# Strassen products for pairs of token chunks in a fused attention and Mish MLP kernel

## The chip, the cores and the metric

One core of a Trainium2 chip. The metric is the device time of one execution in microseconds (us), as the median of several runs. A core has TensorE (PE, matmuls; PEld is its weight load), VectorE (DVE), ScalarE (ACT), GpSimd (POOL) and SyncE (SP, which here only issues DMAs), 16 DMA engines, the on-chip memory SBUF and the matmul result memory PSUM (8 banks of 128 x 512 f32).

## The reference

```python
scores = scale * q @ k.T + bias          # 8 batches, 8 heads, 576 tokens, head size 64
mask = (rel >= 0) & (rel < 128)          # a sliding window of 128 tokens
attn = softmax(where(mask, scores, -1e9))
x = (attn @ v), heads side by side       # 4608 tokens x 512
h = x @ w_in                             # 512 x 2048, float64 weights
g = h * tanh(softplus(h))                # Mish
return g @ w_out                         # 2048 x 512, float64 weights
```

## The kernel before, in words

The 4608 tokens are nine chunks of 512: the first 512 tokens of each of the eight batches (chunks 0 to 7), and chunk 8 of the eight left-over groups of 64. A chunk c has a **first product** (`first`, L407), h = x W_in, in eight pieces j of 256 of the 2048 columns: each is a PSUM tile `h` of [128, 2, 512] with tag "s" (two such buffers, four banks), filled by 24 matmuls and emptied by one ScalarE Mish into `g`. It has a **second product** (`second`, L459), g W_out, in 2 halves x 8 pieces x 2 row blocks of six matmuls each, accumulated in PSUM `po0` and `po1` and stored by `store` (L472).

For precision every operand is a sum of a high and a low part (float32r): a product is three passes, high x high, high x low, low x high. The parts of x come from `split_hi` on ScalarE and `split_lo` on VectorE (L277, L282), those of g from `parts` (L425: ScalarE's high part, GpSimd's low part). W_in and W_out come as float64 words and are turned into parts once, during chunk 0's first product (`sign_w`, `bits_w`, `high_w`, `low_w`, L149 to L174: ScalarE, VectorE, ScalarE, VectorE); all parts then stay in SBUF, in tiles `wi0` to `wi7` and `wo0` to `wo7` of 8 KB per partition.

Attention of a batch is four head pairs p, each with two `unit`s (halves, L185) and a `last_unit` (L302, the 64 left-over tokens). A unit goes through `scores` (PE), `peak` (VectorE: window and maximum), `exps` (ScalarE), `sums` (VectorE), `scale` (GpSimd), `weights` (PE transposes, then VectorE's masking copy), `values` (PE), then the split of x. The left-over tokens go to DRAM (`xs`) and come back as chunk 8 (`last_x`, L391).

Every engine runs its instructions in the order in which they are emitted (`InOrder`, L20). That order is written by hand: lists of (time, step) are sorted by time and emitted. From chunk 1 on, the first product of a chunk stands alone (L523 to L528); beside its 32 steps of the second product (integer times, six matmuls each) stand the attention steps of the next chunk (L543 to L544), four head pairs eight steps apart, at the times that `unit` returns (L296 to L300), multiplied by 4:

```python
(0, scores), (0.02 + t, peak), (0.026 + 27 * t, exps), (0.27 + 33 * t, sums),
(0.33 + 33 * t, scale), (1.53, weights), (1.99, values), (2.02, split_hi), (2.02, split_lo),
```

so that six steps of the second product stand between a unit's scores and its transposes. Loads and stores are issued on SP in the same manner.

Of the kernel before, what the change touches and what calls it, by code (L numbers as in the profile page):

```python
# [16 lines left out]
P = 128  # L17
# [20 lines left out]
def attention_mish_mlp(  # L38
# [132 lines left out]
    def low_w(kind, j):  # L171
        ready.add((kind, j))
        w, t = wt[(kind, j)], wv.pop((kind, j))
        dve.tensor_tensor(out=w[:, 1, :], in0=t, in1=w[:, 0, :].bitcast(F32), op=ALU.subtract)  # L174
# [3 lines left out]
        n = 256 if kind == "i" else DM  # L178
        return wt[(kind, j)][:, part, c * n : c * n + n]

    xt = {}

    HEAD = [slice(i * D, (i + 1) * D) for i in range(2)]

    def unit(b, p, half):  # L185

# [88 lines left out]
                        skip_group_check=True,  # L275
                    )
        def split_hi():  # L277
            if half == 1:
                x = xt[(b, p)] = xp.tile([P, 2, CH], F32R, tag=f"x{p}", name=f"x{b}_{p}")
                act.activation(x[:, 0, :], qkv[("o", b, p)], AF.Copy)  # L280

        def split_lo():  # L282
            if half == 1:
# [12 lines left out]
        t = 0.01 * half  # L296
# [5 lines left out]
    def last_unit(b, p):  # L302

        st = {}
        name = f"{b}_{p}l"
# [61 lines left out]
        if b == 0:  # L367
# [2 lines left out]
                (2.19, keep),  # L370
            ]
        return [
            (0.01, scores), (0.04, peak), (0.31, exps), (0.5, sums), (0.5, scale), (1.54, weights), (1.995, values), (1.996, keep),
        ]

    def attention(b):

        steps = []
        for p in range(NP):
            units = [(2 * p, unit(b, p, 0)), (2 * p, last_unit(b, p)), (2 * p + (b == 0), unit(b, p, 1))]
            steps += [(k + d, f) for k, u in units for d, f in u]
            nxt = (b, p + 2) if p + 2 < NP else (b + 1, p + 2 - NP)
            if 0 < nxt[0] < B:
                steps.append((2 * p + 1.03, lambda nxt=nxt: load_qk(*nxt)))
                steps.append((2 * p + 3.01 - (b > 0), lambda nxt=nxt: load_v(*nxt)))
        return sorted(steps, key=lambda s: s[0])

    def last_x():  # L391
        c = B
        for p in range(NCC):
            raw = at.tile([P, 1024], F32, tag="pz", name=f"xr{p}")[:, :CH]
            sp.dma_start(out=raw, in_=xs[p])
            x = xt[(c, p)] = xp.tile([P, 2, CH], F32R, tag=f"x{p}", name=f"x{c}_{p}")
            act.activation(x[:, 0, :], raw, AF.Copy)
            ready.add((c, p))
            dve.tensor_tensor(
                out=x[:, 1, :], in0=raw, in1=x[:, 0, :].bitcast(F32), op=ALU.subtract  # L400
            )

    gt = {}

# [15 lines left out]

    gs = {}

    def parts(c, half, j):  # L425
# [4 lines left out]
        act.activation(gh, src, AF.Copy)  # L430
        pool.tensor_tensor(out=gl, in0=src, in1=gh.bitcast(F32), op=ALU.subtract)
        gs[(c, half, j)] = (gh, gl)

    po = {}

# [35 lines left out]

    def store(c, half, t):  # L472
        ob = out_tile(c, half, t)
        queues = [sp, sp]
        if (c, half, t) == (B, 1, 1):
            queues = [sp, act]
            act.activation(ob[:, : DM // 2], po[t][:, : DM // 2], AF.Copy)
            dve.tensor_copy(ob[:, DM // 2 :], po[t][:, DM // 2 :])
        elif t == 0:
            dve.tensor_copy(ob, po[t])  # L480
        else:
            act.activation(ob, po[t], AF.Copy)
        for q, (k, rows) in zip(queues, rows_of(c, 2 * half + t)):
            q.dma_start(out=rows, in_=ob[k])

    ORDER = [("i", j) for j in range(NJ)] + [("o", j) for j in range(NJ)]
    LATE = ORDER[-1:]
# [3 lines left out]

    UNIT, START, SLOT = 4.1, 4.7, 5.45
    X0 = START + 9.0 * UNIT
    steps = [(START + UNIT * t, f) for t, f in attention(0)]
# [25 lines left out]
    for _, work in sorted(steps, key=lambda s: s[0]):  # L520
        work()

    for c in range(B + 1):  # L523
        for j in range(NJ if c else 0):
            if j == NJ - 1:
                parts(c, 0, 0)
                parts(c, 0, 1)
            first(c, j)()  # L528

        n = 4 * NJ  # L530
        steps = []
        for m in range(2 * NJ):
            for t in range(2):
                steps.append((2 * m + t, lambda m=m, t=t: second(c, *divmod(m, NJ), t)))
                if m % NJ == NJ - 1:
                    late = 2 if m == n // 2 - 1 and c + 1 < B else 0
                    steps.append((2 * m + t + late, lambda m=m, t=t: store(c, m // NJ, t)))
            if m >= 2:
                steps.append((2 * m - 4.1, lambda m=m: parts(c, *divmod(m, NJ))))
        for w, times in zip(LATE, ((2.3, 8.4, 8.5, 8.9),) if c == 0 else ()):  # L540
            for f, t in zip((sign_w, bits_w, high_w, low_w), times):
                steps.append((t, lambda f=f, w=w: f(*w)))
        if c + 1 < B:  # L543
            steps += [(4 * s + 0.8, f) for s, f in attention(c + 1)]  # L544
        elif c + 1 == B:
            steps.append((4.5, last_x))
        for _, work in sorted(steps, key=lambda s: s[0]):
            work()


_INS = ["q", "k", "v", "moe_w_in", "moe_w_out"]
# [82 lines left out]
```

## Time and profile before

| | us |
|---|---|
| median of 3 runs | 988.91 (988.65 to 989.43) |
| the profiled execution | 988.93 |
| its span, first to last instruction | 987.2 |
| PE busy in the span | 974.5 |

The profile is of one execution; the time of the execution is its span and some 1.7 us around it. "Busy" counts the time in which an engine executes, and matmuls overlap in PE's pipeline. Rows name line 30 for nearly all work, since a helper there records every operation: go by tile names (`h` first product, `po` second product, `s`, `o`, `pt` attention, `gs` parts of g, `si` and `so` parts of the weights, `pz` a unit's exponentials).

### The profile page before, as it was taken

The numbers are of one execution on the slowest core, as the hardware profiler recorded it, in microseconds if no ns is written. First come the engines' busy times: TensorE is split into PE (matmuls) and PEld (weight loads), VectorE is DVE, ScalarE is ACT, GpSimd is POOL, SyncE is SP. The second block draws the span as 40 slices with busy tenths as digits, with TensorE's granted clock in tenths as the row PEclk, the third lists the DMA queues.
The fourth block names the chain that finished last, engine by engine and source line by source line (L and its number), as shares of the span: only waits on it lengthen the run. The fifth ranks groups of instructions, "written<-read, shape, count | busy, mean of one in ns | idle before, by whom it ended". The sixth has DMA issues, their size and how long they took to land.

```text
span 987.2 us, 13729 instructions
## 1 busy us (share of the span) xinstructions
PE 974.5 (99%) x5325; PEld 786.2 (80%) x5329; DVE 322.6 (33%) x1120; ACT 361.2 (37%) x900; POOL 256.0 (26%) x228
## 2 busy tenths in 40 slices
PE   8999999999999999999999999999999999999998
PEld 4678788888888888888888888888888888888886
DVE  6889651044401541055302540145204440000000
ACT  4785541244314332253314531344124431331221
POOL 3210540035103340144104330154004510250142
PEclk9999999999999999999999999999999999999999
DMA  9930131012200221021200310013101110000001
GB/s 374 426 153 28 53 94 37 1 52 81 78 1 27 78 69 37 1 69 65 76 1 28 105 54 25 26 54 95 37 0 51 55 46 1 22 22 21 1 11 33
DMA packets 23393, 61.31 MB, mean 62 GB/s; under 512 B 6688, under 2 KB 7840, under 8 KB 21280
## 3 DMA queue, kind: packets, MB, share of 16 engines
q1 hardware_dynamic: 22016, 59.65, 17.7%
q8 instruction: 42, 0.69, 0.3%
q10 hardware_dynamic: 1312, 0.79, 0.3%
q14 instruction: 23, 0.19, 0.1%
HBM read 49.94 MB, written 10.49 MB: 61 GB/s over the span
## 4 chain that ended last, share of the span: by engine, by line
PE 91%; DVE 4%; ACT 2%; issue 2%; POOL 0%; POOLq 0%; DVEq 0%; ACTq 0%
PE po L30 39%; PE h L30 35%; PE s L30 8%; PE o L30 5%; PE pt_1l L30 1%; PE pt_2l L30 1%; DVE so L30 1%; PE pt_3l L30 1%; DVE ti L30 1%; PE pt_0l L30 1%; DVE to L30 1%; DVE si L30 1%; PE idle L30 1%; ACT wo L30 1%; DVE pz L30 1%
## 5 line engine op out<-in xcount | busy, mean ns | idle before, releaser
L30 PE MATMUL po<-so,gs 128*128 128x512 f32 x1728 | 409.7, 393 | 0.0
L30 PE MATMUL h<-x,si 128*128 128x512 f32 x1728 | 395.3, 390 | 1.6 <-DVE si L30 0.9
L30 PEld LDWEIGHTS h<-x,si 128*128 128x128 f32 x1728 | 323.4, 188 | 70.6 <-DVE si L30 1.7
L30 PEld LDWEIGHTS po<-so,gs 128*128 128x128 f32 x1728 | 320.4, 188 | 65.5
L30 POOL TENSOR_TENSOR gs<-g,gs 128x512 fp32r<-128x512 f32 x144 | 186.3, 1300 | 674.2 <-ACT gs L30 651.3
L30 ACT ACTIVATE g<-h 128x1024 f32<-128x1024 f32 x72 | 74.0, 1027 | 268.2 <-PE h L30 268.2
L30 ACT ACTIVATE gs<-g 128x512 fp32r<-128x512 f32 x144 | 89.4, 628 | 130.7 <-PE po L30 130.7
L30 DVE COPY_PREDICATED s<-older,s 128x256 f32<-128x256 uint16 x64 | 35.6, 557 | 276.6 <-PE s L30 276.6
L30 ACT ACTIVATE pz<-pz,mx 128x128 f32<-128x128 f32 x256 | 99.5, 391 | 44.8 <-DVE mx L30 43.9
L30 DVE TENSOR_TENSOR pz<-s,masks 128x1024 f32<-128x1024 f32 x56 | 66.0, 1219 | 70.1 <-PE s L30 69.6
L30 POOL TENSOR_TENSOR pz<-pz,sm 128x512 f32<-128x512 f32 x64 | 66.7, 1042 | 37.9 <-DVE sm L30 27.6
L30 DVE CUSTOM_DVE_ANT_0 pz<-s,nb 128x128 f32<-128x128 f32 x256 | 59.1, 287 | 2.8
L30 PE MATMUL s<-qk 64*128 64x256 f32 (+1 forms) x512 | 59.1, 368 | 0.0
L30 DVE COPY ob<-po 128x512 f32<-128x512 f32 (+1 forms) x19 | 12.8, 674 | 136.6 <-PE po L30 135.5
L30 ACT ACTIVATE x<-o 128x512 fp32r<-128x512 f32 x32 | 19.0, 594 | 102.2 <-PE o L30 102.2
L30 PE MATMUL o<-pz,va 128*64 128x128 f32 (+1 forms) x560 | 48.7, 320 | 0.0
L30 ACT ACTIVATION_READ_ACCUMULATOR pz<-pz,mx 128x1 f32 x256 | 48.3, 189 | 0.0
L30 PEld LDWEIGHTS s<-qk 64*128 64x128 f32 x512 | 41.6, 189 | 8.3 <-issue 2.1
L30 PEld LDWEIGHTS o<-pz,va 128*64 128x64 f32 x560 | 33.7, 136 | 18.2 <-issue 7.5
L30 PE MATMUL s<-ident,pz 128*128 128x128 f32 x256 | 34.4, 274 | 1.8 <-POOL pz L30 1.8
L30 PEld LDWEIGHTS s<-ident,pz 128*128 128x128 f32 x256 | 29.4, 141 | 7.4 <-POOL pz L30 3.0
L30 ACT ACT_TABLE_LOAD x17 | 21.8, 1283 | 11.2 <-DVE mx L30 11.1
(118 smaller groups left out, 371.4 us busy)
## 6 DMA issues: line engine op xcount, KB each, us to landing
qk<-in_qk_dram SPq DMA_DIRECT2D x31, 640.0 KB, 4.7
va<-in_v_dram SPq DMA_DIRECT2D x28, 320.0 KB, 3.1
wi<-in_moe_w_in_dram SPq DMA_DIRECT2D x8, 1024.0 KB, 12.5
wo<-in_moe_w_out_dram SPq DMA_DIRECT2D x8, 1024.0 KB, 19.9
out_dram<-ob SPq DMA_DIRECT2D x32, 256.0 KB, 2.0
qk<-in_v_dram SPq DMA_DIRECT2D x4, 320.0 KB, 5.8
xr<-xs SPq DMA_DIRECT2D x4, 256.0 KB, 2.7
out_dram<-ob SPq DMA_DIRECT2D x7, 128.0 KB, 2.3
```

Source lines behind the costliest of these rows:

```text
L30: ins = method(*args, **kwargs)
```

## The change

The first products of chunks 1 to 8 are made for pairs (1,2), (3,4), (5,6), (7,8). With X cut into the two chunks and two halves of its 512 features, and W_in into two halves of each side, the eight block products become seven (Strassen's scheme in Winograd's form): X11 W11, X12 W21, four products of sums, and one of a sum with W22. Each is 8 column blocks of 128 x 2 row blocks x 3 passes of matmuls of 128x512. Results are combined as they are evicted (`product`). The W_in sums S1 to S4 are made once, by GpSimd, from W_in parts written to DRAM during chunk 0; all W_in operands of the products are then streamed from DRAM, in 1 MB tiles, through three SBUF buffers per pair. The rest of the W_in tiles become result buffers. Chunk b of a pair keeps its x unsplit (`raw_x`) for the sums. Attention of both chunks of a pair stands beside the second products of the pair before; those of chunks 1 and 2 both stand beside chunk 0's second product and the first two products, with their own times (`FORM[0]`). The diff, cut:

```diff
@@ weights and split
+        elif kind == "i" and j in (3, 5, 7):
+            t = ff.tile([P, 1024], F32, tag="g", name=f"t{kind}{j}", bufs=3)
...
+        if kind == "i" and j > 1:
+            (act if j < 4 else sp).dma_start(out=whole[j], in_=t)      # in bits_w
...
+            if half == 1 and b in raw_x:
+                act.activation(raw_x[b][:, p, :], qkv[("o", b, p)], AF.Copy)
...
-            (0, scores), (0.02 + t, peak), (0.026 + 27 * t, exps), (0.27 + 33 * t, sums),
-            (0.33 + 33 * t, scale), (1.53, weights), (1.99, values), (2.02, split_hi), (2.02, split_lo),
+            (0.8, scores), (0.88 + 0.04 * t, peak), (0.9 + 1.08 * t, exps), (total[half], sums),
+            (total[half] + 0.01, scale), (turn[half], weights), (give[half], values), (give[half] + 0.12, split_hi),
+            (low, split_lo),
...
+        if w[0] == "i":
+            steps.append((lows[n] + 2, lambda j=w[1]: sp.dma_start(out=wr[j], in_=wt[("i", j)].bitcast(F32))))
@@ the pairs
+    PAIRS = [(c, c + 1) for c in range(1, B + 1, 2)]
+    FORM = [   # starts of the head pairs, then turn, give, total, low
+        ((0, 5, 11, 16, 22, 27, 33, 38), (3.15, 4.05), (5.14, 5.16), (0.94, 3.0, 3.1), 6.6),
+        (range(0, 64, 8), (6.92, 6.92), (8.76, 8.78), (1.88, 3.2, 2.8), 8.9),
+    ]
+    COMBINE = (
+        (4.95, 5.3, 5.35, 9.15, 9.4, 14.3, 10.3, 15.15, 16.75, 15.2, 15.95, 17.55),
...
+    )
+    WHOLE = ((4.15, 4.2), (9.2, 9.95))
+    PARTS = (0.1, 3.7, 5.0, 5.5, 8.9, 10.9, 11.5, 15.0, 16.3, 19.7, 21.0, 22.5, 25.1, 26.6)
+    PROD = ["11", "12", "S1", "S2", "S4", "S3", "22"]
...
+    def whole_w(j, k):                       # 4 calls
+        pool.tensor_tensor(out=cw[j][:, 0, k], in0=cw[j][:, 0, k], in1=cw[j][:, 1, k], op=ALU.add)
+    def combine(j):                          # j 0 to 3: four adds, two high, four low, two saves
+        def add(out, x, y, op):
+            pool.tensor_tensor(out=out, in0=x, in1=y, op=op)
+        def high(w):
+            act.activation(w[:, 0, :].bitcast(F32R), w[:, 1, :], AF.Copy)
+        def low(w, k):
+            pool.tensor_tensor(out=w[:, 1, k].bitcast(F32R), in0=w[:, 1, k], in1=w[:, 0, k], op=ALU.subtract)
+        def save(k, w, d):
+            sp.dma_start(out=wc[(k, j // 2)][:, j % 2], in_=w[:, :, d * CH : (d + 1) * CH])
...
+    def load_c(s, n):                        # tile n of 14
+            t = stream[(s, n)] = wts.tile([P, 2, 2, CH], F32R, tag=f"wi{((0, 4, 1) if s else (0, 1, 5))[n % 3]}", name=f"st{s}_{n}")
+            if k in ("11", "12", "22"):
+                for i in range(2):
+                    sp.dma_start(out=t[:, i].bitcast(F32), in_=wr[j][:, :, d * CH : (d + 1) * CH])
+            else:
+                sp.dma_start(out=t.bitcast(F32), in_=wc[(k, q)])
...
+    def product(s, k, i, n):                 # n column blocks of product k
+        if s == 0 and k < 2:
+            h = ps.tile([P, CH], F32, tag=f"po{i % 2}", name=f"m{s}_{k}_{i}").rearrange("p (f n) -> p f n", f=1)
+        else:
+            h = ps.tile([P, 2, CH], F32, tag="s", name=f"m{s}_{k}_{i}", bufs=2)
+        for t in range(n):
+            for d in range(2):
+                for m, (w_, x_) in enumerate(((0, 0), (1, 0), (0, 1))):
+                    pe.matmul(
+                        h[:, t], lhsT=w[:, (i + t) % 4 // 2, w_, 256 * d + (i + t) % 2 * P :][:, :P], rhs=x[:, x_, :],
+                        start=(d + m == 0), stop=(d == 1 and m == 2),
+                    )
+        if (i + n) % 4 == 0 and (s, k, i) != (0, 1, 3):
+            load_c(s, 2 * k + i // 4 + 3)
+        return {
+            0: [(0, lambda: act.activation(A, h, AF.Copy))],
+            1: [(0, lambda: op(dve, Bs, h, A, ALU.add)), (0.6, lambda: mish(Bs))],
+            2: [(0, lambda: act.activation(C, h, AF.Copy))],
+            3: [(0, lambda: op(dve, A, h, A, ALU.add)), (0.1, lambda: op(pool, D, A, C, ALU.add))],
+            4: [(0, lambda: op(dve, D, h, D, ALU.add)), (0.6, lambda: mish(D))],
+            5: [(0, lambda: op(dve, A, h, A, ALU.add)), (0.1, lambda: op(pool, C, A, C, ALU.add)),
+                (2.5, lambda: mish(C))],
+            6: [(0, lambda: op(dve, A, A, h, ALU.subtract)), (0.6, lambda: mish(A))],
+        }[k]
@@ the order: a stage is the second products of a pair (b, then a; L = 64 steps) or of chunk 0 (L = 32), then
@@ the next pair's seven products at L + 8 k + i
+            starts, *form = FORM[s > 0]
+            work += attention(a, starts[:NP], *form)
+            work += attention(b, starts[NP:], *form)          # not for chunk 8: its x is loaded at L - 20
+            for n in range(3):
+                put(L - 8 + n if s else (20, 30, 33)[n], load_c, s, n)
+            # sums of x (sums_x, VectorE) and their parts (split_x, ScalarE and VectorE) at L + 2 to L + 40.2
+                n = 1 if s == 0 and k < 2 else 2
+                for i in range(0, NF // 2, n):
+                    put(L + 8 * k + i, go)
```

Comments in the diff are added here. `FORM` gives the times of a head pair after its start, in steps: `turn` the transposes of its two halves, `give` their values, `total` the sums and scalings, `low` the low part of x. `PARTS`, `WHOLE` and `COMBINE` are the times of the parts of chunk 0's g, and of GpSimd's, ScalarE's and SP's work on the W_in sums, in the steps of chunk 0's second product. Chunk 0's own first product, all second products and the attention's arithmetic are unchanged.

## Rows read from the trace of the kernel before

**Rows 1.** The page of the profile: busy us of each engine, with its share of the span and its instructions, and the chain that ended last by engine.

```profile
PE 974.5 (99%) x5325; PEld 786.2 (80%) x5329; DVE 322.6 (33%) x1120; ACT 361.2 (37%) x900; POOL 256.0 (26%) x228
...
PE 91%; DVE 4%; ACT 2%; issue 2%; POOL 0%; POOLq 0%; DVEq 0%; ACTq 0%
```

**Rows 2.** The engine windows, one line for each stretch (chunk 0's attention and loads; chunk 0's first product; chunk 0's second product with chunk 1's attention; a later first product; a later second product with attention): us, then busy us (and instructions) of PE, PEld, DVE, ACT and POOL, the granted clock, the DMA share and GB/s.

```profile
0.00:43.30 43.30, 38.02 (x273) 22.40 (x277) 32.53 (x126) 26.52 (x89) 13.32 (x28) 1.00 0.97 396
43.30:89.65 46.35, 44.74 (x195) 35.84 (x193) 41.11 (x41) 32.81 (x36) 3.73 (x2) 1.00 0.34 138
89.65:156.20 66.55, 65.47 (x422) 52.38 (x420) 41.77 (x140) 31.33 (x97) 26.55 (x22) 1.00 0.21 65
...
264.85:308.60 43.75, 43.75 (x195) 36.24 (x194) 0.92 (x2) 10.45 (x12) 2.52 (x2) 1.00 0.07 21
308.60:373.50 64.90, 64.90 (x422) 52.35 (x420) 32.36 (x132) 27.58 (x93) 26.00 (x22) 1.00 0.21 66
```

**Rows 3.** The chain that ended last, in order of time: start us, us, what, and how many instructions were merged. A first product, the last first product, the last second product.

```profile
264.88 43.75 PE h L30 x192
...
895.46 43.52 PE h L30 x192
938.98 43.53 PE po L30 x192
```

**Rows 4.** Groups of instructions with shapes kept apart, whole kernel: engine, operation, out<-in by names, out<-in (partitions x elements, type), count | busy us, mean ns of one | idle before them.

```profile
L30 POOL TENSOR_TENSOR gs<-g,gs 128x512 fp32r<-128x512 f32 x144 | 186.3, 1300 | 674.2 <-ACT gs L30 651.3 <-issue 22.9
L30 ACT ACTIVATE gs<-g 128x512 fp32r<-128x512 f32 x144 | 89.4, 628 | 130.7 <-PE po L30 130.7
L30 ACT ACTIVATE g<-h 128x1024 f32<-128x1024 f32 x72 | 74.0, 1027 | 268.2 <-PE h L30 268.2
L30 POOL TENSOR_TENSOR pz<-pz,sm 128x512 f32<-128x512 f32 x64 | 66.7, 1042 | 37.9 <-DVE sm L30 27.6 <-DVE pt_0l L30 5.8 <-DVE pt_3l L30 2.8
L30 DVE TENSOR_TENSOR pz<-s,masks 128x1024 f32<-128x1024 f32 x56 | 66.0, 1219 | 70.1 <-PE s L30 69.6 <-PE pt_0l L30 0.5
...
L30 DVE TENSOR_TENSOR x<-o,x 128x512 fp32r<-128x512 f32 x32 | 22.1, 691 | 6.8 <-ACT x L30 6.8
...
L30 ACT ACTIVATE x<-o 128x512 fp32r<-128x512 f32 x32 | 19.0, 594 | 102.2 <-PE o L30 102.2
...
L30 DVE TENSOR_TENSOR so<-to,so 128x1024 fp32r<-128x1024 f32 x8 | 9.8, 1220 | 0.1
...
L30 ACT ACTIVATE si<-ti 128x1024 fp32r<-128x1024 f32 x8 | 8.3, 1056 | 4.9 <-DVE ti L30 4.9
```

**Rows 5.** DMA issues: out<-in, queue, count, KB each, median us from issue to landing.

```profile
qk<-in_qk_dram SPq DMA_DIRECT2D x31, 640.0 KB, 4.7
va<-in_v_dram SPq DMA_DIRECT2D x28, 320.0 KB, 3.1
...
wo<-in_moe_w_out_dram SPq DMA_DIRECT2D x8, 1024.0 KB, 19.9
```

**Rows 6.** The timeline of chunk 0's head: start us, us, engine, operation, and in brackets the idle time before it and its releaser. First a DMA issue on ScalarE's queue, then the stretch in which ScalarE's high part of the third block of W_in, VectorE's low part and PE follow one another.

```profile
4.23 0.38 ACTq L30 DMA_DIRECT2D nb<-in_relb_dram  x1
...
53.93 1.99 ACT L30 ACTIVATE si<-ti 128x1024 fp32r<-128x1024 f32 x2
55.01 1.23 DVE L30 TENSOR_TENSOR si<-ti,si 128x1024 fp32r<-128x1024 f32 x1 [1.45 <-ACT si L30]
...
56.29 10.72 PE L30 MATMUL h<-x,si 128*128 128x512 f32 x46 [0.53 <-DVE si L30]
```

**Rows 7.** The timeline of the first attention unit of chunk 1, on all engines: scores, VectorE's last work on W_out, the first exponentials' sums, the two scalings and the transposes on PE.

```profile
91.10 1.79 PE L30 MATMUL s<-qk 64*128 64x128 f32 x16
92.56 2.49 DVE L30 TENSOR_TENSOR so<-to,so 128x1024 fp32r<-128x1024 f32 x2
94.98 0.42 DVE L30 COPY_PREDICATED s<-older,s 128x256 f32<-128x256 uint16 x1
...
98.81 0.17 DVE L30 TENSOR_SCALAR sm<-sm 128x4 f32<-128x4 f32 x1 [0.40 <-ACT pz L30]
99.02 0.18 DVE L30 RECIPROCAL sm<-sm 128x4 f32<-128x4 f32 x1
...
100.62 1.05 POOL L30 TENSOR_TENSOR pz<-pz,sm 128x512 f32<-128x512 f32 x1
...
102.38 1.04 POOL L30 TENSOR_TENSOR pz<-pz,sm 128x512 f32<-128x512 f32 x1 [0.70 <-ACT wo L30]
...
103.47 0.66 PE L30 MATMUL s<-ident,pz 128*128 128x128 f32 x4 [1.08 <-POOL pz L30]
```

**Rows 8.** VectorE and GpSimd at the same time: the timeline of VectorE from 62.38 and of GpSimd at 63.97, and over the whole kernel the min/median/max ns of GpSimd's two groups.

```profile
62.38 1.23 DVE L30 TENSOR_TENSOR si<-ti,si 128x1024 fp32r<-128x1024 f32 x1 [1.02 <-ACT si L30]
...
64.37 2.21 DVE L30 SCALAR_TENSOR_TENSOR ti<-wi,ti 128x1024 uint32<-128x1024 uint32 x1
66.49 2.29 DVE L30 TENSOR_TENSOR si<-ti,si 128x1024 fp32r<-128x1024 f32 x1
...
63.97 3.73 POOL L30 TENSOR_TENSOR gs<-g,gs 128x512 fp32r<-128x512 f32 x2 [24.65 <-ACT gs L30]
...
L30 POOL TENSOR_TENSOR gs<-g,gs x144: 1266/1290/2256, 64.0 to 975.1; 128x512 fp32r<-128x512 f32 x144
L30 POOL TENSOR_TENSOR pz<-pz,sm x64: 1036/1042/1050, 9.2 to 800.9; 128x512 f32<-128x512 f32 x64
```

More of the change, by code (lines that the diff above doesn't have):

```diff
@@ L179, in w_part, with unit @@
         return wt[(kind, j)][:, part, c * n : c * n + n]
-    xt = {}
+    whole = [dram.tile([P, 1024], F32, tag=f"wt{j}", name=f"wt{j}") for j in range(NJ)]
+    wr = [dram.tile([P, 2, 1024], F32, tag=f"wr{j}", name=f"wr{j}") for j in range(NJ)]
+    xt, raw_x = {}, {}
     HEAD = [slice(i * D, (i + 1) * D) for i in range(2)]
-    def unit(b, p, half):
+    def unit(b, p, half, turn=(0, 0), give=(0, 0), total=(0, 0), low=0):
         st = {}
@@ L282, in split_lo @@
         def split_lo():
-            if half == 1:
+            if half == 1 and b not in raw_x:
                 x = xt[(b, p)]
@@ L372, in last_unit, with loads, attention0, attention @@
         return [
-            (0.01, scores), (0.04, peak), (0.31, exps), (0.5, sums), (0.5, scale), (1.54, weights), (1.995, values), (1.996, keep),
-        ]
-    def attention(b):
+            (0.84, scores), (0.96, peak), (2.04, exps), (total[2], sums), (total[2], scale),
+            (turn[1] + 0.04, weights), (give[1] + 0.02, values), (give[1] + 0.024, keep),
+        ]
+    def loads(b, p):
+        nxt = (b, p + 2) if p + 2 < NP else (b + 1, p + 2 - NP)
+        if 0 < nxt[0] < B:
+            return [lambda: load_qk(*nxt), lambda: load_v(*nxt)]
+        return []
+    def attention0():
         steps = []
         for p in range(NP):
-            units = [(2 * p, unit(b, p, 0)), (2 * p, last_unit(b, p)), (2 * p + (b == 0), unit(b, p, 1))]
+            units = [(2 * p, unit(0, p, 0)), (2 * p, last_unit(0, p)), (2 * p + 1, unit(0, p, 1))]
             steps += [(k + d, f) for k, u in units for d, f in u]
[L385 to L401, printed above, removed]
+            steps += [(2 * p + d, f) for d, f in zip((1.03, 3.01), loads(0, p))]
+        return steps
+    def attention(b, starts, *form):
+        steps = []
+        for p in range(NP):
+            k = starts[p]
+            for u in (unit(b, p, 0, *form), last_unit(b, p, *form), unit(b, p, 1, *form)):
+                steps += [(k + d, f) for d, f in u]
+            steps += [(k + d, f) for d, f in zip((4.9, form[1][1] + 0.06), loads(b, p))]
+        return steps
     gt = {}
@@ L473, in store @@
         ob = out_tile(c, half, t)
[L474 to L479, printed above, removed]
+        if (c, half, t) == (B - 1, 1, 1):
+            rows = rows_of(c, 2 * half + t)[0][1]
+            m = DM // 2
+            act.activation(ob[:, :m], po[t][:, :m], AF.Copy)
+            dve.tensor_copy(ob[:, m:], po[t][:, m:])
+            act.dma_start(out=rows[:, :m], in_=ob[:, :m])
+            sp.dma_start(out=rows[:, m:], in_=ob[:, m:])
+            return
+        if t == 0:
             dve.tensor_copy(ob, po[t])
@@ L482, in store @@
             act.activation(ob, po[t], AF.Copy)
-        for q, (k, rows) in zip(queues, rows_of(c, 2 * half + t)):
-            q.dma_start(out=rows, in_=ob[k])
+        for k, rows in rows_of(c, 2 * half + t):
+            sp.dma_start(out=rows, in_=ob[k])
     ORDER = [("i", j) for j in range(NJ)] + [("o", j) for j in range(NJ)]
@@ L493, in attention_mish_mlp @@
     X0 = START + 9.0 * UNIT
-    steps = [(START + UNIT * t, f) for t, f in attention(0)]
+    steps = [(START + UNIT * t, f) for t, f in attention0()]
     idles = [(0, 0.63, 6), (2 * NP - 1, 0.78, 4)] + [(k, 1.31, 4) for k in range(2 * NP)]
@@ L521, in attention_mish_mlp @@
         work()
[L523 to L548, printed above, removed]
+    PAIRS = [(c, c + 1) for c in range(1, B + 1, 2)]
@@ new lines, in attention_mish_mlp, with fetch_w @@
+    wc = {
+        (k, q): dram.tile([P, 2, 2, CH], F32, tag=f"wc{k}{q}", name=f"wc{k}{q}") for k in PROD[2:6] for q in range(2)
+    }
+    cw = {}
+    def fetch_w(j):
+        cw[j] = wts.tile([P, 2, 1024], F32, tag=f"wi{j}", name=f"cw{j}")
+        if j > 1:
+            sp.dma_start(out=cw[j][:, 0, :], in_=whole[j])
+        else:
+            sp.dma_start(out=cw[j], in_=wr[j])
+    def whole_w(j, k):
+        pool.tensor_tensor(out=cw[j][:, 0, k], in0=cw[j][:, 0, k], in1=cw[j][:, 1, k], op=ALU.add)
@@ new lines, in attention_mish_mlp, with sums_x, new, op @@
+    comb = {}
+    def sums_x(s, what):
+        a, b = PAIRS[s]
+        raw = raw_x[b]
+        def new(k):
+            comb[(s, k)] = ff.tile([P, 2, CH], F32, tag="g", name=f"{k}{s}", bufs=3)
+            return comb[(s, k)]
+        def op(out, x, y, o):
+            dve.tensor_tensor(out=out, in0=x, in1=y, op=o)
+        if what[:2] == "T1":
+            t = comb[(s, "T1")] if what == "T1b" else new("T1")
+            for k in {"T1a": (0,), "T1b": (1,)}.get(what, range(2)):
+                op(t[:, k], raw[:, k], xt[(a, k)][:, 0].bitcast(F32), ALU.subtract)
+                op(t[:, k], t[:, k], xt[(a, k)][:, 1].bitcast(F32), ALU.subtract)
+        elif what == "T4":
+            t = new("T4")
+            for k in range(2):
+                op(t[:, k], comb[(s, "T1")][:, k], xt[(a, 2 + k)][:, 0].bitcast(F32), ALU.add)
+                op(t[:, k], t[:, k], xt[(a, 2 + k)][:, 1].bitcast(F32), ALU.add)
+        elif what == "T2":
+            t = comb[(s, "T2")] = comb[(s, "T1")]
+            for k in range(2):
+                op(t[:, k], raw[:, 2 + k], t[:, k], ALU.subtract)
+        elif what == "T4b":
+            t = comb[(s, "T4")]
+            op(t, raw[:, 2:], t, ALU.subtract)
+        elif what == "T3":
+            op(raw[:, :2], raw[:, 2:], raw[:, :2], ALU.subtract)
+            comb[(s, "T3")] = raw[:, :2]
```

159 lines of the change are left out of this document (147 added, 12 removed), and 3 rows, old and new, of the table COMBINE.

## The prediction

> **What bounds the kernel now.** I read the page's busy shares and its chain first: TensorE is busy 99% of the span and makes up 91% of the chain [rows 1]. No other engine passes 37%, but those are averages, so next come the engine windows by stage [rows 2]. A first product of one chunk (264.85 to 308.60) keeps PE busy for all of its 43.75 us, with ScalarE at 10.4, VectorE at 0.9 and GpSimd at 2.5. A second product with the next chunk's attention beside it (308.60 to 373.50) also has PE busy throughout: 64.90 us. Only two stages hold idle PE time: chunk 0's first product (46.35 us, 44.74 busy, VectorE at 41.11) and chunk 0's second product (66.55 us against the usual 64.90). So a matmul taken out of a full stage is worth its own pitch, unless the stage then finds another limit. The pitch: 192 matmuls of 128x512 in 43.75 us on the chain, 227.9 ns each [rows 3]. The durations of single matmuls overlap in the pipeline and aren't used.
>
> **The change part by part.**
>
> *Fewer matmuls.* Two chunks cost 2 x 192 = 384 first-product matmuls now. Seven products x 8 column blocks x 2 row blocks x 3 passes is 336. Four pairs save 192 matmuls; at 227.9 ns that is 43.75 us, and at the 43.52 us of the last first product [rows 3] it would be 43.5. I take -43.7 us. Second products, attention and chunk 0 keep their matmuls, and each new matmul has the old shape, so the pitch stays.
>
> *Evictions.* A [128, 2, 512] result is filled by 12 matmuls, 2.73 us; there are two such buffers. It was 24 matmuls, emptied by one Mish of 1027 ns. Now 8 of a pair's 28 results go out by a ScalarE copy (nearest row the 1027 ns again) and 20 by a VectorE add of a PSUM and an SBUF operand, nearest the 1219 ns mask multiply [rows 4]. Both are under 2.73 us. Over the 76.6 us of the seven products VectorE has 20 x 1.22, some 20 half-size sums and splits at 0.69, and 2 full-size ones at 1.22: 41 us, 53%. ScalarE has 24 x 1.03 plus 10 x 0.59: 31 us. GpSimd has 8 adds of double width, 2 x 1.30 each: 21 us. Cost zero, bounded above by 0.5 us per pair for a late hand-over at the seam, 2 us in all. PE is the cover of each: if an evictor slips past 2.73 us, PE waits for the bank.
>
> *Streaming W_in.* Each pair reads 14 tiles of 1 MB, one per 24 matmuls, 5.47 us, or 192 GB/s. A tile is requested when the one three places ahead of it has been used up, so it has two tiles, 10.9 us, to land. Nearest rows: 640 KB lands in 4.7 us and 320 KB in 3.1 [rows 5], so 1 MB lands in 6.6 us by the line through both, or 7.5 in proportion to the larger. The 16 engines together moved 396 GB/s in the first 43 us [rows 2], which is 2.65 us per tile. All are under 10.9: zero. The requests stand on SP, which waits for PE there; behind them in the product stage stand only other tiles, and the output stores, which nothing waits for.
>
> *Chunk 0's head.* VectorE turns W_in into parts here and paces the stage. Added are 14 stores (11 MB): 12 on SP, which computes nothing, and two (blocks 2 and 3) on ScalarE. There a DMA issue takes about 0.38 us [rows 6], and it waits for VectorE's bits, ahead of Mish and the split that VectorE itself awaits (VectorE sat 1.45 us for it at 55.01, and PE then 0.53 [rows 6]). That is 2 x 0.38 = +0.8 us, between 0 and 2: the high end if both issues also wait a VectorE operation. SP's qk and v loads for chunk 1 stand behind some stores, which wait for VectorE; they are not used before 91 us, and landed in 5 [rows 5], so zero.
>
> *Chunk 0's second product with two attentions.* This is the dense place. PE has 32 steps of six matmuls and the first 12 of product one and two, 44 x 1.367 = 60.1 us, and twice the attention's 64.90 - 43.53 = 21.4: 103 us in place of 64.9 and what followed. GpSimd has 14 low parts and 36 sums and low parts of W at 1.30 (nearest row of the two-input kind), and 16 scalings at 1.04 [rows 4]: 81.6 us, 79%. VectorE has 2 x 32.4 plus 10 to 15; ScalarE has 27.6 now, of which 8.8 are 14 parts at 0.63, so 2 x 18.8 plus these 8.8, 8 splits of W at 1.06 and 13 us of copies and Mish: some 70. Throughput fits; latency is the question.
>
> The first attention unit: today its scores start at 91.10, VectorE is busy with W_out until 94.98, GpSimd scales at 100.62, and PE, which had six steps in between, still waits 1.08 us [rows 7]. The new list puts three steps between scores and transposes. The transposes would be due 97.4: 89.65, one step, 2.3 us of scores, three steps. The scaled half is ready at about 100.4: sums at 98.81, 0.4 for both small operations, 0.1, 1.04. PE loses 3.0 us, the old 1.08 goes: +1.9. What follows gains from that: the second half's exponentials, scaling and transposes are then in time.
>
> The second unit: between the scaling of unit one and that of unit two stand eight GpSimd operations, 8 x 1.30 = 10.4 us. Counted from 101.8 (first unit's second scaling) the next scaled half is ready at 113.3; PE, with transposes, two steps' worth of values and scores and four steps, wants it at 113.0. VectorE's conversion of the last W_out block lies in the same stretch, and there the two engines slow each other: a VectorE operation of two SBUF operands took 2.21 and 2.29 us in place of 1.23 beside two GpSimd ones that took 3.73 together in place of 2.6 [rows 8]. I take +1.0, between 0 and 3.
> Units three to eight have four to seven GpSimd operations in such a gap, and three of the six gaps are a step longer: +1.5 together, between 0 and 10. What the stage lost beside the 1.08 (66.55 - 64.90 - 1.08 = 0.57) is left as it is.
> The loads this stage adds are 5 MB of W at its start: at 396 GB/s 13 us, the first of them wanted by GpSimd only at 101.8. SP's stores of W sums wait for GpSimd; behind them stand the qk and v loads of a unit two places on, some 25 us ahead of use. Zero for both.
>
> The rule that speaks against the change: the Trainium skill (SBUF: State Buffer, "Who interferes with whom") has VectorE and GpSimd share one port pair under an exclusive lock when VectorE reads two SBUF operands, so the later one waits for the whole of the other's operation; the 2.2 us rows fit that. Attention's VectorE work reads PSUM on one side, and the scalings beside it stayed within 1036 to 1050 ns [rows 8], so by rows and rule alike only W_out's last block and the sums of x collide; were every operation to collide, the second rival would follow.
>
> *Sum.* The profiled execution took 988.93 us (span 987.2 plus 1.7 around it), the median of the runs 988.91: the same. 988.9 - 43.7 + 0.8 + 1.9 + 1.0 + 1.5 = 950.4; call it **950.5 us**. Low ends give 988.9 - 43.7 - 1.0, the last where first-unit waits vanish too: 944.5. High ends without a rival: 988.9 - 43.5 + 2 + 2 + 1.9 + 3 + 10 = 964.
>
> **Rivals.**
> 1. *The dense stage hides everything.* VectorE may be free earlier, and units wait for nothing: 988.9 - 43.7 = 945.2. For it: PE loses nothing in any later attention stage [rows 2]. Against: today's 1.08 us there with twice the steps. 0.13.
> 2. *GpSimd becomes the bound in that stage.* If its 50 two-input operations take not 1.30 but the 2.26 us of its worst row [rows 8], it needs 81.6 + 48 = 130 us where PE needs 103: 27 us lost, 945.2 + 27 = 972; with half of them, 958 or less. For: 79% load already. Against: the median of 144 such operations is 1.29. 0.17.
> 3. *Slower: the stream of W tiles sets the pace.* It decides once a tile takes over 5.47 us of the queue, and the whole is slower than before once it takes 39 / 56 = 0.7 us more, 6.2 us. If tiles land one after another at the 7.5 us scaled above, 56 x 2.05 = 115 us are added: 1065. For: W_out's 1 MB took 19.9 us to land, in a queue of eight [rows 5]. Against: that queue moved 396 GB/s. The Trainium skill (DMA: Bandwidth & Descriptors, "Measured") gives 6.15 us for a 1 MB transfer by itself, about the break-even, an estimate of 988 us if tiles never overlapped. 0.06.
> 4. *The saving isn't there*, as the pitch grows with the new operand order (high, low, high): 192 matmuls must come back as 14% of pitch. No row hints at it. 0.02.
>
> **How the numbers follow.** My forecast, 946 to 957, has 0.62, with rivals 0.13, 0.17, 0.06, 0.02. The range 944.5 to 964 leaves out rivals 3 and 4 and the upper half of 2, some 0.16. A measurement here tells about 0.2%, 2 us, from no change. Faster 0.92 (forecast, 1, 2), same 0.02, slower 0.06.
>
> **What would show it.** Right: 1344 streamed matmuls plus 192 old ones in the first product; each pair's seven products in 76 to 77 us with PE full; PE's idle time collected between 90 and 195 us, released by GpSimd or VectorE on the transposes; the tiles landing in 4 to 8 us. Wrong: PE waiting for tile loads, or for the two result banks in any pair; GpSimd over 90% busy from 90 to 190 us; a first product of chunk 0 longer by over 2 us.

## The result and the profile after

The changed kernel takes 964.61 us (median; 963.73 to 965.57), against 988.9: ratio 0.9754, 95% interval 0.9737 to 0.9771. It is faster, by 24.3 us, where 38.4 were forecast, and lies 0.6 us above the range. Its profiled execution is one of 964.61 us.

The page after, for [rows 1] and [rows 5]: busy us of the engines, the chain by engine, and the two groups of tile loads.

```profile
PE 938.8 (97%) x5137; PEld 752.9 (78%) x5137; DVE 493.5 (51%) x1276; ACT 417.4 (43%) x978; POOL 381.3 (40%) x296
...
PE 81%; DVE 3%; ACT 1%; issue 0%; POOL 0%; POOLq 0%
...
st<-wcS SPq DMA_DIRECT2D x32, 1024.0 KB, 4.8
st<-wr SPq DMA_DIRECT2D x48, 512.0 KB, 5.6
```

GpSimd's load grew from 26% to 40% of a shorter span. The chain's 81% for PE can't be held against the 91% of before: followed back, it breaks off at 137.95 us, and its shares add up to only 85% of the span, nearly all of it PE. The 1 MB tiles of W_in sums land in 4.8 us, the others in two halves of 5.6, and no row has PE wait for them. PE's waits, the four largest sums by releaser (times and longest behind each):

```profile
PE h L30 <- ACT si L30: 6.3, 1, 6.3
PE s L30 <- POOL pz L30: 4.4, 4, 2.3
PE m L30 <- DVE B L30: 2.5, 2, 1.9
PE m L30 <- DVE D L30: 1.6, 4, 0.4
```

Where the time went is found by laying stages side by side. First a later stage, the second products of chunks 2 and 1 and the products of pair (3,4), on PE:

```profile
272.58 1.52 PE L30 MATMUL po<-so,gs 128*128 128x512 f32 x6
...
400.52 2.91 PE L30 MATMUL m<-x,st 128*128 128x512 f32 x12
...
452.22 5.74 PE L30 MATMUL m<-x,st 128*128 128x512 f32 x24 [0.41 <-DVE D L30]
...
479.56 1.52 PE L30 MATMUL po<-so,gs 128*128 128x512 f32 x6
```

From 272.58 to 479.56 are 207.0 us. Two second products (2 x 43.52), eight attention units (8 x 5.345; a unit is here a head pair, a quarter of the 64.90 - 43.52 us that one batch took before) and 336 matmuls at 227.9 ns are 206.4. So a later pair loses 0.6 us, of which 0.41 is the wait before 452.22; three pairs lose under 2. The saving of 43.7 us is there, and 19.4 us of it are then given back, nearly all at two places ahead of 272.58. The windows, for [rows 2]: chunk 0's first product, then three stretches that follow a wait of PE.

```profile
42.94:96.67 53.73, 47.00 (x195) 37.54 (x194) 41.20 (x41) 33.45 (x35) 3.23 (x2) 0.94 0.98 399
...
61.12:66.00 4.88, 4.84 (x11) 3.35 (x12) 4.17 (x4) 4.85 (x5) 0.00 (x0) 0.50 1.01 420
107.00:112.50 5.50, 5.49 (x21) 4.28 (x21) 3.24 (x8) 2.28 (x5) 4.71 (x4) 0.69 0.01 1
213.00:217.45 4.45, 4.45 (x13) 3.49 (x13) 3.47 (x6) 0.00 (x1) 0.00 (x0) 0.62 1.08 334
```

Chunk 0's first product, the head, takes 53.73 us where it took 46.35; it starts 0.4 us earlier, so 7.0 us are lost. From its end at 96.67 to 272.58 are 175.9 us, where a second product, two attentions and seven products are 43.5 + 42.8 + 76.6 = 162.9 without loss: 13.0 are lost, of which 1.65 was lost before too. And 7.0 for the head, 11.4 more here than before, and 1.2 for the later stages (three waits of 0.41) are 19.6, where the kernel misses 945.2 by 19.4 us.

The head's wait, on all engines (SPq and ACTq are the issues of DMAs), answering [rows 6]:

```profile
43.31 0.33 SPq L30 DMA_DIRECT2D qk<-in_qk_dram  x1
...
57.42 0.35 ACTq L30 DMA_DIRECT2D wt<-ti  x1
57.80 1.28 ACT L30 ACT_TABLE_LOAD   x1 [6.50 <-DMA qk<-in_qk_dram]
...
61.10 1.23 DVE L30 TENSOR_TENSOR si<-ti,si 128x1024 fp32r<-128x1024 f32 x1 [7.93 <-ACT si L30]
61.12 11.23 PE L30 MATMUL h<-x,si 128*128 128x512 f32 x36 [6.33 <-ACT si L30]
```

ScalarE stood 6.50 us ahead of the Mish, until a load of qk issued by SP at 43.31 had landed (the longest qk load took 14.0 us), and only then issued its store at 57.42. Behind it were Mish and the high parts, so VectorE waited 7.93 us and PE 6.33, and from 61.12 to 66 PE had half its clock (0.50 of 2.4 GHz). The compiled program explains who waits for whom: it hands eight completion semaphores (counters that tell that a DMA has landed) to its DMAs in turn, and a DMA is issued only when the one eight places before it has landed. Eight places before this store stands that load; the trace has seven DMA issues between the two.

In the stage that follows, the first attention unit, lines of the second to fourth, and the seam of the first pair (where its second product is evicted while VectorE makes sums T of x), answering [rows 7]:

```profile
107.01 0.67 PE L30 MATMUL s<-ident,pz 128*128 128x128 f32 x4 [2.33 <-POOL pz L30]
107.42 2.82 PE L30 MATMUL po<-so,gs 128*128 128x512 f32 x6
...
116.78 0.66 PE L30 MATMUL pt_1l<-qk 128*128 128x128 f32 x4 [0.58 <-DVE xo_0l L30]
...
129.15 1.79 PE L30 MATMUL s<-qk 64*128 64x128 f32 x16
...
137.99 0.65 PE L30 MATMUL s<-ident,pz 128*128 128x128 f32 x4 [0.45 <-POOL pz L30]
...
141.98 1.79 PE L30 MATMUL s<-qk 64*128 64x128 f32 x16
...
154.14 1.66 PE L30 MATMUL po<-so,gs 128*128 128x512 f32 x6
...
206.33 5.46 POOL L30 TENSOR_TENSOR cw<-cw 128x512 fp32r<-128x512 f32 x4 [1.17 <-ACT cw L30]
...
208.94 1.72 DVE L30 TENSOR_TENSOR T<-raw,x 128x512 f32<-128x512 f32 x1
...
210.69 1.65 DVE L30 TENSOR_TENSOR T<-T,x 128x512 f32<-128x512 f32 x1
...
213.00 4.61 PE L30 MATMUL m<-x,st 128*128 128x512 f32 x12 [1.88 <-DVE B L30]
```

PE waited 2.33 us at 107.01 (in the waits above), and the six matmuls behind it took 2.82 us, not 1.64. At 208.94 VectorE's two sums T took 1.72 and 1.65 us where one of that size takes 0.69, as GpSimd ran four low parts of W_in sums beside them; an eviction of product two stood behind them, PE waited 1.88 us and its next 12 matmuls took 4.61 us instead of 3.04.

### The profile page after: what moved, and what is told of

It reads as the page before. It is cut to its first block, busy times and chain, and to the rows that moved or that the text cites. A ratio compares the mean times of both kernels' runs of the same rounds, so it can differ in the third digit from the quotient of the medians.

```text
span 962.9 us, 14049 instructions
## 1 busy us (share of the span) xinstructions
PE 938.8 (97%) x5137; PEld 752.9 (78%) x5137; DVE 493.5 (51%) x1276; ACT 417.4 (43%) x978; POOL 381.3 (40%) x296
## 3 DMA queue, kind: packets, MB, share of 16 engines
q10 hardware_dynamic: 1664, 1.84, 0.5%
## 4 chain that ended last, share of the span: by engine, by line
PE 81%; DVE 3%; ACT 1%; issue 0%; POOL 0%; POOLq 0%
PE po L30 39%; PE m L30 29%; PE s L30 7%; PE o L30 5%; DVE xT L30 1%; PE pt_3l L30 1%; PE pt_2l L30 1%; PE pt_1l L30 1%; PE pt_0l L30 1%; DVE D L30 0%; ACT pz L30 0%; DVE pz L30 0%; POOL pz L30 0%; ACT cw L30 0%; DVE B L30 0%
## 5 line engine op out<-in xcount | busy, mean ns | idle before, releaser
L30 PE MATMUL m<-xT,st 128*128 128x512 f32 x768 | 175.4, 389 | 0.0
L30 PEld LDWEIGHTS m<-xT,st 128*128 128x128 f32 x768 | 144.2, 188 | 30.0
L30 PE MATMUL m<-x,st 128*128 128x512 f32 x576 | 138.1, 396 | 4.3 <-DVE B L30 2.5
L30 PEld LDWEIGHTS m<-x,st 128*128 128x128 f32 x576 | 108.0, 190 | 29.5 <-DVE D L30 3.3
L30 POOL TENSOR_TENSOR C<-A,C 128x1024 f32<-128x1024 f32 x16 | 38.4, 2400 | 50.2 <-DVE A L30 49.9
L30 POOL TENSOR_TENSOR gs<-D,gs 128x512 fp32r<-128x512 f32 x32 | 41.1, 1289 | 43.0 <-ACT gs L30 43.0
L30 POOL TENSOR_TENSOR gs<-B,gs 128x512 fp32r<-128x512 f32 x32 | 41.0, 1287 | 33.6 <-ACT gs L30 33.4
L30 POOL TENSOR_TENSOR gs<-A,gs 128x512 fp32r<-128x512 f32 x32 | 41.2, 1289 | 32.0 <-ACT gs L30 31.8
L30 PE MATMUL h<-x,si 128*128 128x512 f32 x192 | 47.2, 407 | 6.7 <-ACT si L30 6.3
L30 POOL TENSOR_TENSOR gs<-C,gs 128x512 fp32r<-128x512 f32 x32 | 41.0, 1289 | 23.2 <-ACT gs L30 23.2
L30 PEld LDWEIGHTS h<-x,si 128*128 128x128 f32 x192 | 37.4, 197 | 16.3 <-ACT si L30 6.8
## 6 DMA issues: line engine op xcount, KB each, us to landing
wo<-in_moe_w_out_dram SPq DMA_DIRECT2D x8, 1024.0 KB, 19.6
```

What stands on the lines that cost most here:

```text
L30: ins = method(*args, **kwargs)
```

## The experiments

Two questions were put. What made the head's 7 us: a DMA issue on a computing engine that waits for an older transfer, or the fuller queue itself? And what made the waits behind it: VectorE and GpSimd in each other's way, the order of the operations on one of them, or the length of GpSimd's queue? The letters of the theories are those of the expectations. All times are medians; the kernel before ran beside each, at 988.6 to 988.8. Differences are against the kernel that an edit starts from.

**Stores on SP.** In `bits_w`:

```diff
-            (act if j < 4 else sp).dma_start(out=whole[j], in_=t)
+            sp.dma_start(out=whole[j], in_=t)
```

> Only edit: the two stores of W_in blocks 2 and 3 are issued on SP instead of ScalarE. Theory A (the store waits on ScalarE for an older load, and Mish and the high parts stand behind it): chunk 0's first product falls from 53.7 us to 46.5 to 49, PE's 6.3 us wait and the half-clock stretch behind it (clock 0.50 from 61 to 66 us) are gone, total about 958 to 960. Theory B (the DMA engines, busy 0.98 of that stage at 399 GB/s, are what the stage waits for, wherever the store is issued): the first product stays at 52 to 54 us and the total at 964 to 965.

Measured: 964.34 us, the head 54.2 us. A's forecast failed and B's numbers came, for another reason: ScalarE no longer waits ahead of the Mish, but VectorE waits 8.88 us for a buffer (the profile names no releaser), and PE behind it:

```profile
68.11 0.69 DVE L30 TENSOR_SCALAR ti<-wi 128x1024 uint32<-128x1024 uint32 x1 [8.88 <-issue]
...
73.54 24.18 PE L30 MATMUL h<-x,si 128*128 128x512 f32 x96 [6.52 <-ACT g L30]
```

The instruction is the first of block 5, and in the compiled program it waits until the store of block 3 has landed, which reads the buffer that block 5 is to get; DMAs to and from these DRAM tiles landed up to 10.7 us after their issue, and three of the stores were issued from 57.03 on. In the next kernel, which lacks the two stores, block 5 does not wait at all; block 7 waits 1.71 us, and PE loses nothing behind it. This run alone leaves A and B open.

**Without the two whole stores.** Blocks 2 and 3 are not stored whole; GpSimd sums their parts again in the next stage, as it does for 0 and 1.

```diff
-        if kind == "i" and j > 1:
-            (act if j < 4 else sp).dma_start(out=whole[j], in_=t)
+        if kind == "i" and j > 3:
+            sp.dma_start(out=whole[j], in_=t)
...
-    WHOLE = ((4.15, 4.2), (9.2, 9.95))
+    WHOLE = ((4.15, 4.2), (9.2, 9.95), (22.51, 22.52), (31.0, 32.35))
...
```

> Only edit: blocks 2 and 3 of W_in are not stored whole; their sums of high and low part are made again on GpSimd in the next stage (4 more operations of 1.3 us), as for blocks 0 and 1. Theory A: as with the stores on SP, 46.5 to 48 us for chunk 0's first product, and no wait of VectorE for buffers held by the two stores; the later stage at most 1 us longer; total 957 to 959. Theory B: 1 MB less of 19 MB changes the first product by at most 1 us; total 964 to 966, since GpSimd has 5.2 us more to do.

Measured: 959.46 us, -5.2. The head's window:

```profile
43.34:89.64 46.30, 44.67 (x195) 35.85 (x193) 39.42 (x40) 32.63 (x34) 3.58 (x2) 1.00 1.02 422
```

46.30 us, the old time, with the DMA engines as full as before (1.02, 422 GB/s). So the full queue by itself costs this stage nothing; a computing engine that waits for something in it does. B is out. But the next stage lost more: PE's wait for the first unit grew to 3.02 us, and both waits were followed by slow matmuls:

```profile
101.83 0.70 PE L30 MATMUL s<-ident,pz 128*128 128x128 f32 x4 [3.02 <-POOL pz L30]
102.24 2.86 PE L30 MATMUL po<-so,gs 128*128 128x512 f32 x6
...
207.77 4.60 PE L30 MATMUL m<-x,st 128*128 128x512 f32 x12 [1.85 <-DVE B L30]
```

**The stores alone**, put into the kernel before, with the buffers and DRAM tiles that they need and nothing else of the change:

```diff
+        if kind == "i" and j > 1:
+            (act if j < 4 else sp).dma_start(out=whole[j], in_=t)
...
+        if w[0] == "i":
+            steps.append((lows[n] + 2, lambda j=w[1]: sp.dma_start(out=wr[j], in_=wt[("i", j)].bitcast(F32))))
```

> The kernel before with one part of the change alone: the 14 stores of chunk 0's head (two of them on ScalarE), nothing reads them. Theory A (the stores' waits on ScalarE and the buffers they hold cost the head its 7 us): chunk 0's first product 53 to 54 us in place of 46.35, total 995 to 997. Rival (the head was lengthened by something else in the change, such as another placement of tiles): at most 1 us more than before, 989 to 990.

Measured: 995.61 us, +6.8 (ratio 1.0071, 1.0056 to 1.0086), with ScalarE's 5.55 us and PE's 5.41 at the same place. The profiled execution is the shortest, 994.83; its head, from 43.22 to 95.01, takes 51.8 us, 5.4 more than before, where A's forecast was 53 to 54. The loss is not the same in every execution: the two edits below that leave the head of the changed kernel as it is show 53.4 and 51.9 us, with PE waiting 5.79 and 4.89. So the stores alone make the wait and, within this spread, its size; that something else in the change lengthened the head is out.

```profile
43.22 6.21 PE L30 MATMUL h<-x,si 128*128 128x512 f32 x26
...
57.15 1.28 ACT L30 ACT_TABLE_LOAD   x1 [5.55 <-DMA qk<-in_qk_dram]
...
60.46 2.05 PE L30 MATMUL h<-x,si 128*128 128x512 f32 x3 [5.41 <-ACT si L30]
...
95.01 1.52 PE L30 MATMUL po<-so,gs 128*128 128x512 f32 x6
```

**GpSimd's last low parts later.** In `COMBINE`, last row:

```diff
-        42.5, 43.0, 42.95, 43.3, 44.9, 43.35, 43.38, 44.98),
+        42.5, 43.0, 42.95, 43.3, 44.9, 49.5, 49.6, 51.0),
```

> Only edit: GpSimd's last two W_in low parts (5.5 us of work for four are in one block at 206 us) come some 6 steps later, so that two of four no longer run while VectorE makes the sum T1. Theory C (VectorE's two sums of two SBUF operands took 1.72 and 1.65 us for 0.69, as GpSimd runs beside them; the PSUM bank of product two waits behind them): the sums fall to 0.7 to 1.2 us, PE's 1.9 us wait at 213 us to under 1, the half-clock stretch behind it goes; total 961 to 963. Theory D (the order on VectorE alone, two sums between two evictions, makes the wait): the wait stays over 1.5 us, total within 1 us of 964.6.

Measured: 963.48 us, and the wait still 1.87. It tells nothing on C: a later place in the list delays no instruction whose engine has nothing else to do, and GpSimd ran the same four low parts back to back at the same point (from 207.09, 5.45 us).

**One T1 sum behind an eviction.** In `sums_x`, the second subtraction of T1b becomes a step of its own at L + 12.65.

```diff
                 op(t[:, k], raw[:, k], xt[(a, k)][:, 0].bitcast(F32), ALU.subtract)
-                op(t[:, k], t[:, k], xt[(a, k)][:, 1].bitcast(F32), ALU.subtract)
+                if what != "T1b":
+                    op(t[:, k], t[:, k], xt[(a, k)][:, 1].bitcast(F32), ALU.subtract)
```

> Only edit: the second of VectorE's two T1 sums is emitted one eviction later, so that one sum instead of two stands ahead of the eviction of product two's fifth block; GpSimd's work stays. Theory D (order on VectorE): PE's wait at 213 us falls from 1.9 to at most 0.4 us, the clock stays full there, total 961 to 962.5. Theory C (contention with GpSimd): the sums still take some 1.7 us each, the wait falls only by half or moves to the next bank; total 963 to 964.5.

Measured: 964.09 us. The 1.88 us became 0.20, 1.42 for the next bank and 1.20 for ScalarE's copy of C, and the time is within 0.5 us of the changed kernel's: D is out, order alone moves the wait.

**GpSimd held back.** On the kernel without the two whole stores, ScalarE's high part is put later, so GpSimd's last two low parts can't start.

```diff
-        42.5, 43.0, 42.95, 43.3, 44.9, 43.35, 43.38, 44.98),
+        42.5, 45.3, 42.95, 43.3, 44.9, 45.35, 45.38, 46.98),
```

> On top of the kernel without the two whole stores (959.5): ScalarE makes the high part of the last W_in sum pair later, so that GpSimd can't start the last two low parts while VectorE makes T1 (the earlier edit of their place alone left GpSimd running them at once, since nothing held it back). Theory C (contention): at least the second T1 sum takes 0.7 us in place of 1.65, PE's 1.85 us wait for the bank falls to about 0.9, total 957.5 to 958.5. Theory D (VectorE simply has too much in that stretch): the later split and eviction wait instead, total 959 to 960.

Measured: 957.11 us (956.5 to 959.4), -2.35, and C holds: both sums T take 0.68 and 0.69 us where the kernel that this edit starts from has 1.67 and 1.65, and the 1.85 us wait is gone; in its place stands one of 0.72 for a tile load (the kernel with the stores on SP has it too, 0.77, so the later place of a store need not be its cause).

```profile
101.91 0.66 PE L30 MATMUL s<-ident,pz 128*128 128x128 f32 x4 [3.02 <-POOL pz L30]
102.32 1.64 PE L30 MATMUL po<-so,gs 128*128 128x512 f32 x6
...
104.96 5.18 POOL L30 TENSOR_TENSOR cw<-cw 128x512 f32<-128x512 f32 x3
...
106.84 2.18 DVE L30 SCALAR_TENSOR_TENSOR to<-wo,to 128x1024 uint32<-128x1024 uint32 x1
...
116.18 0.66 PE L30 MATMUL s<-ident,pz 128*128 128x128 f32 x4 [1.84 <-POOL pz L30]
...
203.38 0.68 DVE L30 TENSOR_TENSOR T<-raw,x 128x512 f32<-128x512 f32 x1
204.10 0.69 DVE L30 TENSOR_TENSOR T<-T,x 128x512 f32<-128x512 f32 x1
...
215.07 16.82 PE L30 MATMUL m<-xT,st 128*128 128x512 f32 x72 [0.72 <-DMA st<-wcS]
```

The same kernel shows the two attention waits: 3.02 us (behind which, here, six matmuls took 1.64 at a granted clock of 1.00), and 1.84 at 116.18, behind GpSimd's queue, whose three sums took 5.18 us, not 3 x 1.29 = 3.9, beside VectorE's conversion, which took 2.18 where it takes 1.23 alone.

**W_out's last but one block later too.** On the kernel without the two whole stores:

```diff
-    LATE = ORDER[-1:]
+    LATE = ORDER[-2:]
...
+            for w, times in zip(LATE, ((0.85, 1.0, 2.1, 3.3), (3.6, 5.0, 8.0, 9.4))):
```

> On top of the kernel without the two whole stores (959.5): the last but one block of W_out is also turned into parts in the next stage, behind the first attention unit's window and maximum, so VectorE reaches that unit some 3 us sooner. Theory E (VectorE's conversion backlog is what PE's first 3.0 us wait is made of, and the half clock right behind it costs 1.4 us more): the wait at 101.8 us falls to under 0.5 us, the stretch behind it runs at full clock, total 955 to 956.5. Theory F (GpSimd's queue or the three-step spacing itself sets it): the wait stays at 1.5 to 3 us or comes back at the second unit, total 958 to 959.5.

Measured: 960.13 us, +0.7, which the spread of the two kernels' executions covers. The 3.02 us fell to 0.28, and came back further on:

```profile
99.00 0.66 PE L30 MATMUL s<-ident,pz 128*128 128x128 f32 x4 [0.28 <-POOL pz L30]
...
102.27 0.66 PE L30 MATMUL s<-ident,pz 128*128 128x128 f32 x4 [1.23 <-POOL pz L30]
...
116.85 0.66 PE L30 MATMUL s<-ident,pz 128*128 128x128 f32 x4 [2.15 <-POOL pz L30]
```

F holds on the waits, and its total is 0.6 us short: PE reaches the second unit's transposes at 116.85, against 116.18 in the kernel with GpSimd held back, where VectorE is late in the first unit. Taking VectorE out of the way changes only which wait is last.

**Both.** The two last edits together.

> Both edits together on the kernel without the two whole stores. If theories C and E hold: 953.5 to 955.5, with what is left of the loss against 945 in the seam of the first pair and in the finer interleaving of attention. If D and F hold: 958 to 960.

Measured: 958.57 us (957.3 to 960.9), in the range for D and F. The 2.15 us wait is still there, as F has it, and in the profiled execution (960.86, the longest) a wait of 1.7 for the split of T1 is new, as D has it. Holding GpSimd back is worth 1.6 us on top of W_out's late block, not 2.35.

**GpSimd's queue.** On the kernel with GpSimd held back, two of its eight operations go ahead of unit one's scaling; then the same with W_out's block later.

```diff
-    WHOLE = ((4.15, 4.2), (9.2, 9.95), (22.51, 22.52), (31.0, 32.35))
+    WHOLE = ((0.2, 0.3), (9.2, 9.95), (22.51, 22.52), (31.0, 32.35))
```

> On top of the kernel with neither whole stores nor late GpSimd collision (957.1): the first two of the eight GpSimd operations that stand between the scalings of units one and two go ahead of unit one's, into GpSimd's idle time (97.5 to 100.8 us there). Theory G (GpSimd's queue of eight operations makes PE's 1.84 us wait at 116 us): six are left, 2.6 us less, the wait falls to under 0.4 us, total 955 to 956. Rival H (VectorE's and ScalarE's chain through the second unit is as late): the wait stays over 1.2 us, total 956.5 to 957.5.

> The same, with the last but one block of W_out turned into parts behind the first unit's window and maximum. Theory G: now both the first unit's 3.0 us (which went before, but came back as waits of 1.2 and 2.15 us further on) and the second's are gone, total 952.5 to 954.5. Rival H: VectorE's conversion comes back as waits in units one and two, total 955 to 957.

Measured: 956.65 and 955.62 us. In the first the second unit's wait for GpSimd is gone, as G has it, but the first unit's is 3.38 us and PE then has 0.55 of its clock, so little is won (0.5 us, within the spread):

```profile
102.28 1.11 PE L30 MATMUL s<-ident,pz 128*128 128x128 f32 x4 [3.38 <-POOL pz L30]
```

```profile
102.20:106.00 3.80, 3.72 (x13) 3.07 (x14) 2.64 (x6) 1.99 (x3) 3.31 (x4) 0.55 0.00 0
```

In the second the waits are 1.49, 0.98, 0.49 and 1.09 us, the last in unit two for VectorE: smaller and more of them, at full clock. G is right on the second unit's wait for GpSimd, but G's totals are 0.7 and 1.1 us short; both measured totals lie in H's ranges, and in the second kernel VectorE's work does come back as waits in units one and two, as H has it. Neither theory holds alone.

```profile
92.54 1.13 PE L30 MATMUL s<-qk 64*128 64x256 f32 x8 [1.49 <-ACT g L30]
...
99.42 0.66 PE L30 MATMUL s<-ident,pz 128*128 128x128 f32 x4 [0.98 <-POOL pz L30]
...
101.97 0.66 PE L30 MATMUL s<-ident,pz 128*128 128x128 f32 x4 [0.49 <-POOL pz L30]
...
109.58 0.66 PE L30 MATMUL pt_1l<-qk 128*128 128x128 f32 x4 [1.09 <-DVE xo_0l L30]
```

955.62 (ratio 0.9666, 0.9653 to 0.9679) is the fastest version found, 9.0 us under the changed kernel.

## Why the prediction was wrong

- **Fewer matmuls, -43.7**: right, in mechanism and size. Later pairs come to 0.6 us of what 227.9 ns per matmul gives.
- **Evictions and streaming, 0**: right for the later pairs (0.41 us each; tiles in 4.8 us, sooner than the 6.6 to 7.5 that were estimated). For the first pair the eviction term failed: it priced each eviction by its own duration and the seam at 0.5 us at most. There PE lost 0.65 + 1.88 us, and some 1.7 more in the 4.45 us at clock 0.62. I had named the collision of GpSimd with the sums of x and given it no price; with the collision taken away 2.35 us came back. The Trainium skill (SBUF — State Buffer, "Who interferes with whom") has a VectorE instruction with two SBUF inputs and a GpSimd instruction that reads SBUF contend for one shared pair of ports, under an exclusive lock; the traces agree: 1.72 and 1.65 us beside GpSimd, 0.68 and 0.69 without.
- **The head, +0.8, between 0 and 2**: the step that failed. Two ScalarE DMA issues of 0.38 us each counted the issue and a wait for VectorE, and not the wait for an older load in a queue of 399 GB/s. It cost 7.0 us, and the stores alone lengthened the kernel before by 6.8. That an issue can wait so was in the trace of before: SP waited 16.5 us for W_in loads and 16.9 for W_out loads that it had issued itself, only there nothing that computes stood behind it. A first product of chunk 0 longer by over 2 us was one of the signs of being wrong that the prediction named.
- **First unit**: the wait forecast at 3.0 us was 2.33, and 3.02 with the head repaired. What followed it was not priced: in the changed kernel the next 5.5 us ran at clock 0.69, so 1.7 us more.
- **Second unit, +1.0**: the forecast wait for GpSimd did not come in the changed kernel; 0.58 us were lost to VectorE's copy of the left-over tokens instead (`xo_0l`). Where no slow stretch stood ahead of it, the wait for GpSimd came, 1.84 us with GpSimd held back and 1.82 with the stores on SP. That the slow stretch gave GpSimd the time fits this, and is not shown by itself. That 0.58 is near 1.0 is luck, since the mechanism was another.
- **Units three to eight, +1.5**: waits of 0.45 and 0.45 for GpSimd and 0.17 for a result bank. A listed wait is not its whole cost. The fourth unit (141.98 to 154.14), without a wait, takes 12.16 us, and five steps and its attention are 5 x 1.36 + 5.345 = 12.15: finer interleaving costs it nothing, only the lone step behind it (to 155.73) takes 1.59 in place of 1.36. The third (129.15 to 141.98), with 0.45 of wait, takes 12.83: 0.67 more, 0.2 beyond the wait. The sixth (167.89 to 180.70) has the same wait and takes 12.81. For the eight waits of this stage 0.2 each would be 1.6, an estimate from these two units.
- Of the 13.0 us of this stage 6.9 are waits, 3.4 slow clock (1.7 each) and 1.6, by that estimate, what waits cost beyond their listed time; 1.1 stays unexplained, of which three such lone steps would be 0.7. Rival 2 (GpSimd the bound throughout) did not come: it was busy 58 of the first 80.6 us, 72%. Rivals 1, 3 and 4 did not come either.
- The time lies only 0.6 us outside the range, so the head or the seam at its forecast size would have kept it inside; the head is the larger. With it repaired the kernel takes 959.46 us, inside 944.5 to 964, though above the forecast's 957. The low end of the range is 944.2 by the prediction's own terms, not 944.5; it changes nothing.

Still open: whether 945 can be reached. With every named cause treated, the version at 955.62 still has ten waits of PE from 0.2 to 1.5 us between 89 and 213 us.

## What to carry to other kernels

When a bound engine gets less work, price the stages in which its neighbours are full one by one: nearly the whole loss here lay in the two stages where VectorE and GpSimd had most to do, and about 1 us in the other three quarters. A DMA issue on a computing engine can wait for an unrelated older transfer, so put it where nothing stands behind it, and count the time for which its source buffer is held. After removing one wait, look for the next in the same chain before counting the gain.

## What the runs showed of the hardware

- PE's clock: behind waits of 6.33, 2.33 and 1.88 us the granted clock was 0.50, 0.69 and 0.62 of 2.4 GHz over stretches of 4.5 to 5.5 us: the first is its lower level (1.2 GHz), the others lie between its two levels. Behind a wait of 3.02 us it fell in one kernel (six matmuls in 2.86 us) and not in another (1.64). A wait of some 2 us thus cost up to 1.7 us more than it shows, and two kernels that are alike up to that point differ by 1.2 us in six matmuls.
- PE's matmuls lost nothing beside DMA engines at 1.02 busy and 422 GB/s: 46.30 us in place of 46.35.
- VectorE's sums of 128x512 with two SBUF operands took 1.72 and 1.65 us beside GpSimd and 0.68 and 0.69 without; its evictions with one PSUM operand, at 208.34 beside the same GpSimd work, stayed at 0.68.
